# Attention stage: k transposed on TensorE, its high half copied on GpSimd, the first batch's tails turned on TensorE, and the order of the cycle written anew

## The chip, the cores and the metric

One core of one Trainium2 chip runs the whole program. The metric is the device time of one execution in microseconds; the time before is the median of three runs.

## The reference

```
# q, k, v: (2, 8, 576, 64), s: (2, 8, 576)
scores = (q @ k.T) / sqrt(64)
cum    = cumsum(max(s, 0))
bias   = -(cum[:, :, :, None] - cum[:, :, None, :])
scores = where(causal, -1e9, scores + min(bias, 0)); attn = softmax(scores)
x = attn @ v                      # heads side by side: (1152, 512)
h = x @ w_in;  x = (h * cos(h)) @ w_out          # d_ff = 2048
expert = argmax(x @ w_gate); out = gate * (relu(x_e @ w1[e]) @ w2[e])   # 8 experts, F = 1024
```

The change is in the attention stage alone.

## The kernel before

The program has four stages: attention, the first layer (`l1`), the second layer with the routing, and the experts. Float32 products are built from 16-bit parts: a value is split into a high part and a low part, and three products (high x high, high x low, low x high) are added up in PSUM.

Attention works on eight pairs of heads (n = 0 to 7; pairs 0 to 3 are batch 0). A sequence has 576 rows: four full blocks of 128 (`FULL`) and a tail of 64, and the tails of the two heads of a pair share one tile. For the scores, q and k of a pair must lie transposed, in tiles `qT` and `kT` with two chunks. Chunk 0 holds the high part of one operand over the low part (128 rows); chunk 1 holds the high part once more (64 rows) and six bias rows made from the cumulative sum, 70 rows in all (`KB`). The way there, pair by pair: load (`LQK`), split on GpSimd into `parts_` (`K`: a cast for the high part, a subtraction for the low part), transpose by DMA and read the bias rows from a DRAM copy `bt` (`TR`), and copy the high half into chunk 1 by DMA (`DUP`, the function `twice`). The tails of a batch go the same way (`LT`, `KT`, `TT`, `DT`). Pair 0 is different: `a_first` transposes it on TensorE.

The steps of the computation are S (scores), M (mask, scale and row minimum on VectorE), E (exponential on ScalarE), T (transpose of the probabilities on TensorE), C (copy of it out of PSUM), V (times v), N and R (reciprocal of the row sums, spread over the columns by TensorE), X (tail times v), RC, XS, XT, PX (scaling and splitting the result). S4, SD and the steps with 4 in their name treat the tail. Between them stand D, A and W, which decode and load blocks of `w_in` for the first layer.

All engines work through their queues in program order, and the table `CYCLE` is that order: in iteration i, an entry with offset o treats pair i - o. `ONACT` says which copies C run on ScalarE; the others run on VectorE. PSUM has eight banks: two each of "s", "pt", "mm" and "sm".

Of the kernel before, what the change touches and what calls it, by code (L numbers as in the profile page):

```python
# [74 lines left out]
def kernel(ctx, tc, q, k, v, s, w_in, w_out, wg, w1, w2, out, cap, wide):  # L75
# [238 lines left out]
    def pair_more(n):  # L314
        for x, nm in enumerate("qk"):
            twice(att[n][nm + "T"], x)

    def pair_bias(n):
        for x, nm in enumerate("qk"):
            bias_rows(att[n][nm + "T"], x, n, 0, 1, 2 * FULL)  # L320

    def tail_T(ap, b):
        for x, nm in enumerate("qk"):
            tails[b][nm + "T"] = turned(ap, wt[x], nm + "t", NP, 2)

    def tail_more(b):
        for x, nm in enumerate("qk"):
            twice(tails[b][nm + "T"], x)
# [5 lines left out]
    def a_first(ap):  # L334
        d = att[0]
        work_ = (("q", first[0], d["q"], 0), ("k", first[1], d["k"], 1))
        for nm, w_, f, x in work_:
            gate["hi"] = V(nc.scalar.activation, halves(w_[:, 0], x)[0], f, AF.Copy)
        for nm, w_, f, x in work_:
# [991 lines left out]
```

## Time and profile before

| | us |
|---|---|
| median of 3 runs | 466.72 |
| lowest and highest | 463.45, 467.72 |
| the profiled execution | 464.23 |
| its span | 462.4 |
| TensorE matmul, VectorE, ScalarE, GpSimd busy | 411.2, 329.2, 275.8, 127.8 |

The profiled execution's time is 1.83 us longer than its span; times within it are counted from the start of the span. Durations are those of one execution. Busy times of matmuls are modelled at their ends, so neighbouring rows of the time order can overlap a little.

### The profile page before, as it was taken

The numbers are of one execution on the slowest core, as the hardware profiler recorded it, in microseconds if no ns is written. First come the engines' busy times: TensorE is split into PE (matmuls) and PEld (weight loads), VectorE is DVE, ScalarE is ACT, GpSimd is POOL, SyncE is SP. The second block draws the span as 40 slices with busy tenths as digits, with TensorE's granted clock in tenths as the row PEclk, the third lists the DMA queues.
The fourth block names the chain that finished last, engine by engine and source line by source line (L and its number), as shares of the span: only waits on it lengthen the run. The fifth ranks groups of instructions, "written<-read, shape, count | busy, mean of one in ns | idle before, by whom it ended". The sixth has DMA issues, their size and how long they took to land.

```text
span 462.4 us, 10882 instructions
## 1 busy us (share of the span) xinstructions
PE 411.2 (89%) x4032; PEld 288.3 (62%) x4032; DVE 329.2 (71%) x782; ACT 275.8 (60%) x634; POOL 127.8 (28%) x213
## 2 busy tenths in 40 slices
PE   2487988899999897899899999979899999998994
PEld 2256767676765554555444445435698899888962
DVE  6456889899499958988988566466581467667761
ACT  5256786878666766677722543153653576777771
POOL 7533324511244444354520002201002110220221
PEclk9998999999999999999999999989999999998998
DMA  7799988991313995222255756794769678988851
GB/s 162 154 198 182 189 149 172 182 160 48 93 46 103 328 326 179 93 91 69 72 176 183 216 133 133 178 274 123 251 201 237 105 206 310 306 258 283 286 175 45
DMA packets 101208, 81.82 MB, mean 177 GB/s; under 512 B 72834, under 2 KB 81282, under 8 KB 101147
## 3 DMA queue, kind: packets, MB, share of 16 engines
q1 hardware_dynamic: 97835, 76.06, 62.8%
q0 software_dynamic: 2256, 4.73, 3.2%
q8 instruction: 33, 0.54, 0.5%
q10 hardware_dynamic: 1056, 0.26, 0.3%
q14 instruction: 28, 0.23, 0.2%
HBM read 57.67 MB, written 12.36 MB: 151 GB/s over the span
## 4 chain that ended last, share of the span: by engine, by line
PE 32%; DMA 10%; DVE 7%; ACT 3%; issue 3%; POOL 1%; SPq 0%; ACTq 0%; DVEq 0%; POOLq 0%
DMA ws<-in_moe_w_dram 8%; PE ps_mm L813 7%; PE ps_sm L813 4%; PE ps_s L1012 3%; PE ps_pt L990 2%; PE ps_s L990 2%; PE ps_pt L1012 2%; PE ps_mm L990 2%; PE ps_pt L813 2%; PE ps_s L813 2%; PE ps_mm L1012 2%; ACT gall L605 2%; DMA xr<-row 1%; DVE y L764 1%; DVE gall L606 1%
## 5 line engine op out<-in xcount | busy, mean ns | idle before, releaser
L758 PEld LDWEIGHTS <-win 128*128 128x128 f16 x576 | 56.1, 98 | 45.6 <-issue 9.9
L813 PEld LDWEIGHTS <-gall 128*128 128x128 f16 x432 | 41.3, 98 | 50.7 <-issue 4.2
L813 PE MATMUL ps_mm<-wout,gall 128*128 128x512 f16 x240 | 58.0, 387 | 1.3 <-DVE n__2891 L772 1.3
L606 DVE SCALAR_TENSOR_TENSOR gall<-ws,gall 128x1024 f16<-128x1024 f32 x32 | 38.6, 1220 | 21.3 <-ACT gall L605 21.1
L240 ACT ACTIVATE z<-z,st 128x128 f32<-128x128 f32 (+2 forms) x80 | 44.3, 556 | 7.4 <-DVE st L240 7.4
L999 POOL DMA_INDIRECT out_dram<-gall,eM x16 | 20.5, 1282 | 99.1 <-ACT gall L998 90.5
L605 ACT ACTIVATE gall<-ws 128x1024 f16<-128x1024 f32 x32 | 33.6, 1056 | 23.7 <-DMA ws<-in_moe_w_dram 23.6
L240 DVE CUSTOM_DVE_ANT_0 z<-ps_s,zm 128x512 f32<-128x512 f32 (+3 forms) x72 | 34.8, 507 | 14.0 <-PE ps_s L243 13.7
L605 ACT ACTIVATE wout<-ws 128x512 f16<-128x512 f32 (+1 forms) x32 | 27.2, 860 | 26.1 <-DVE ws L636 19.3
L606 DVE SCALAR_TENSOR_TENSOR wout<-ws,wout 128x512 f16<-128x512 f32 (+1 forms) x32 | 30.3, 956 | 9.7 <-ACT wout L605 9.6
L758 PE MATMUL ps_mm<-xT,win 128*128 128x384 f16 x192 | 33.8, 326 | 2.4 <-DVE n__2438 L772 2.0
L758 PE MATMUL ps_s<-xT,win 128*128 128x384 f16 x192 | 34.3, 326 | 1.7 <-DVE n__2257 L772 0.6
L893 POOL DMA_INDIRECT disp<-row,rsli x9 | 9.2, 1021 | 94.6 <-ACT rm L874 48.5
L606 DVE SCALAR_TENSOR_TENSOR win<-ws,win 128x1024 f16<-128x1024 f32 (+1 forms) x27 | 27.1, 1003 | 10.6 <-ACT win L605 10.2
L758 PE MATMUL ps_pt<-xT,win 128*128 128x384 f16 x192 | 33.8, 326 | 0.9 <-DVE n__2555 L772 0.9
L605 ACT ACTIVATE win<-ws 128x1024 f16<-128x1024 f32 (+1 forms) x27 | 24.2, 897 | 16.8 <-DMA ws<-in_moe_w_dram 10.8
L243 PE MATMUL ps_s<-kT,qT 128*128 128x128 f16 (+7 forms) x128 | 26.3, 329 | 5.9 <-DMA kT<-kT 5.2
L246 PE MATMUL ps_pt<-idf,z 128*128 128x128 f32 x192 | 30.0, 289 | 0.1
L240 ACT COPY p<-ps_pt 128x512 f32<-128x512 f32 (+1 forms) x32 | 16.8, 526 | 22.2 <-PE ps_pt L246 21.9
L771 ACT ACTIVATE y<-y,quarter 128x384 f32<-128x384 f32 x48 | 29.1, 606 | 0.0
L990 PEld LDWEIGHTS <-gall 128*128 128x128 f16 x480 | 28.0, 97 | 0.7 <-DVE gall L606 0.5
L246 PEld LDWEIGHTS ps_pt<-idf,z 128*128 128x128 f32 x192 | 22.9, 148 | 5.1 <-issue 2.6
(483 smaller groups left out, 879.6 us busy)
## 6 DMA issues: line engine op xcount, KB each, us to landing
ws<-in_moe_w_dram SPq DMA_DIRECT2D x64, 512.0 KB
ws<-in_moe_w_in_dram SPq DMA_DIRECT2D x16, 512.0 KB
ws<-in_moe_w_out_dram SPq DMA_DIRECT2D x16, 512.0 KB
disp<-zc SPq DMA_DIRECT2D x18, 257.0 KB
out_dram<-zc SPq DMA_DIRECT2D x9, 256.0 KB
qf<-in_q_dram SPq DMA_DIRECT2D x16, 128.0 KB
vf<-in_v_dram SPq DMA_DIRECT2D x16, 128.0 KB
kf<-in_k_dram SPq DMA_DIRECT2D x14, 128.0 KB
```

The costliest lines, as they stand in the source:

```text
L240: return pin(f(*a, **kw))
L243: return pin(nc.tensor.matmul(out_, **kw))
L246: return pin(nc.tensor.transpose(out_, in_, id_))
L605: nc.scalar.activation(hi, src, AF.Copy, scale=sc)
L606: (eng or nc.vector).scalar_tensor_tensor(lo, src, sc, hi, ALU.mult, ALU.subtract)
L758: nc.tensor.matmul(hp[:, 0:CH], lhsT=win[a][:, kk, fs], rhs=xT[:, x_, kk, xs], start=(n == 0), stop=(n == 3 * KD - 1))
L771: nc.scalar.activation(y, y, AF.Sin, scale=TWO_PI, bias=quarter)
L813: gate["pe"] = nc.tensor.matmul(xp, lhsT=G[c][:, a, f, ts], rhs=wout[w_][:, f, :], start=(f == 0 and n == 0), stop=(f == KF - 1 and n == 2))
L893: sc = nc.gpsimd.indirect_dma_start(out=disp, out_offset=bass.IndirectOffsetOnAxis(ap=sli.bitcast(U32), axis=0), in_=r, in_offset=None, bo ...
L990: gate["pe"] = nc.tensor.matmul(hp[:, 0:ns], lhsT=a1[:, kk, a, fs], rhs=X[:, x_ * KD + kk, 0:ns], start=(n == 0), stop=(n == 3 * KD - 1))
L999: sc = nc.gpsimd.indirect_dma_start(out=out, out_offset=bass.IndirectOffsetOnAxis(ap=M[:, b, 1:2].bitcast(U32), axis=0), in_=y, in_offset= ...
L1012: nc.tensor.matmul(yp[:, 0:ns], lhsT=a2[:, f, w_, d * 128:(d + 1) * 128], rhs=Hh[:, a, f, :], start=(n == 0), stop=(n == 3 * KE - 1))
```

## The change

k is no longer transposed by DMA: eight TensorE transposes per pair (`KT`) write one bank of "sm", seen as 1024 16-bit columns, and VectorE copies it to `kT` (`CK`). q stays with the DMA transpose. The second copy of the high half, of q, k and tails, is made by GpSimd instead of DMA. For that the places of the high and the low part are swapped in `halves`, so that q's high part is copied from partitions 64 to 127 and k's from 0 to 63. The tile `kT` has two buffers instead of three. The tails of batch 0 are cast, doubled and transposed in `a_first`, on ScalarE, GpSimd and TensorE, with their bias columns from SBUF; those of batch 1 still go by DMA transpose. The copies C4 and C4b go to ScalarE, and `ONACT` changes. The loads of pair 3 are issued ahead of the loop, and the whole table `CYCLE` is another order.

```
-ONACT = ((0,), (1,), (3, 0), (3, 1))
+ONACT = ((1,), (2, 0), (3, 1))
...
-    ("DUP", -1), ("C", 1, 1), ("DT", -1), ("LQK", -3), ("S", 0, 0, 1), ("S", 0, 0, 0), ("T", 1, 2, 0), ("E4b", 1), ("M", 1, 3, 1),
...
+    ("LQK", -3), ("S", 0, 0, 1), ("C", 1, 2, 1), ("S", 0, 0, 0), ("E", 1, 3, 1), ("S", 0, 1, 0), ("S", 0, 1, 1), ("M4b", 1), ("T", 1, 3, 0),
+    ("PX", 2), ("BK", -1), ("C", 1, 2, 0), ("M", 0, 0, 1), ("M", 0, 0, 0), ("KT", -1), ("E4", 1), ("M", 0, 1, 0), ("C", 1, 3, 0),
...
     def halves(w_, x):
-        return w_[:, :, x, :], w_[:, :, 1 - x, :]
+        return w_[:, :, 1 - x, :], w_[:, :, x, :]
...
     def twice(t, x):
-        V(nc.sync.dma_start, t[0:D, 1], t[x * D:x * D + D, 0])
+        o = (1 - x) * D
+        V(nc.gpsimd.tensor_copy, t[0:D, 1], t[o:o + D, 0])
...
-    def pair_T(ap, n):
-        for x, nm in enumerate("qk"):
-            att[n][nm + "T"] = turned(ap, parts_[x][n % 2], nm, 2 * FULL, PB)
+    def q_T(ap, n):
+        d = att[n]
+        d["qT"] = turned(room(ap, "q", 2 * FULL, PB), parts_[0][n % 2])
+
+    def k_room(ap, n):
+        att[n]["kT"] = room(ap, "k", 2 * FULL, 2)
...
+        for z in tail_:
+            hi_(*z)
+        for z in tail_:
+            lo_(*z)
...
+        for z in tail_:
+            dup_(*z)
+        for c in range(2):
+            for w_, f, x in tail_:
+                turn_(w_, tl["qk"[x] + "T"], c, 0, nc.scalar.copy, i)
+                i += 1
...
     def o_C4(n):
-        V(nc.vector.tensor_copy, d["p4"], d["pt4"])
+        V(nc.scalar.copy, d["p4"], d["pt4"])
...
     def o_TR(n):
         if n > 1:
-            pair_T(pools["ap"], n)
-            pair_bias(n)
+            q_T(pools["ap"], n)
+            pair_bias(n, 0)
+
+    def o_BK(n):
+        if n > 1:
+            k_room(pools["ap"], n)
+            pair_bias(n, 1)
+
+    def o_KT(n):
+        if n:
+            pt = att[n]["ptk"] = bank("sm", 2, F16, 1024)
+            for j in range(2 * FULL):
+                tr_(pt[:, j * 128:(j + 1) * 128], parts_[1][n % 2][:, j].rearrange("p b d -> p (b d)"), idh)
+
+    def o_CK(n):
+        if n:
+            V(nc.vector.tensor_copy, att[n]["kT"][:, 0].rearrange("p a t -> p (a t)"), att[n]["ptk"])
...
+        load(ap, 0, "v", v, 3)
         V(nc.sync.dma_start_transpose, out=bT, in_=bias_)
-        tail_T(ap, 0)
-        load_v(ap, 0)
+        q_T(ap, 1)
+        load_tail(ap, 0, "v", v, 2)
+        wl["load"]()
         V(nc.sync.dma_start, bt[0:NBT * 128, :].rearrange("(b p) t -> p b t", p=128), bT)
-        pair_T(ap, 1)
-        tail_more(0)
-        tail_bias(0)
-        pair_more(1)
-        pair_bias(1)
-        wl["load"]()
+        load_qk(ap, 3)
+        k_room(ap, 1)
+        for x in range(2):
+            pair_bias(1, x)
```

Before, SyncE's queue at the start, behind the first loads (`bT` is the transposed bias block, `wt` the split tails, `parts` the split pair 1):

```order
L240 DMA_TRANSPOSE bT<-bias__101 128x7x128
L240 DMA_TRANSPOSE qtT<-wt_109 128x4x128
L240 DMA_TRANSPOSE ktT<-wt_110 128x4x128
L240 DMA vf<-in_v_dram 128x4x64 x2
L240 DMA vt<-in_v_dram 64x4x64 x2
L240 DMA bt<-bT 128x7x128
L240 DMA_TRANSPOSE qT<-parts_106 128x8x128
L240 DMA_TRANSPOSE kT<-parts_108 128x8x128
L240 DMA qtT<-qtT 64x512
L240 DMA ktT<-ktT 64x512
L240 DMA qtT<-bt 6x4x128
L240 DMA ktT<-bt 6x4x128
```

After, the same place of the same queue, SyncE's at the start:

```order
L240 DMA vf<-in_v_dram 128x4x64 x2
L240 DMA_TRANSPOSE bT<-bias__101 128x7x128
L240 DMA_TRANSPOSE qT<-parts_106 128x8x128
L240 DMA vt<-in_v_dram 64x4x64 x2
L663 DMA ws_91<-in_moe_w_in_dram 128x4x128
L240 DMA bt<-bT 128x7x128
L240 DMA qf<-in_q_dram 128x4x64 x2
L240 DMA kf<-in_k_dram 128x4x64 x2
L240 DMA qT<-bt 6x8x128
L240 DMA kT<-bt 6x8x128
```

Nothing of the tails is left in it; the bias rows of pair 1 stand behind a weight load and the loads of pair 3.

Before, GpSimd in one full cycle (casts and subtractions of the next pair, and the residue of a finished one):

```order
L240 CAST parts_106<-qf 128x8x64
L240 TENSOR_TENSOR parts_106<-qf,parts_106 128x8x64
L240 TENSOR_TENSOR xT<-xs,xT 128x576
L240 CAST parts_108<-kf 128x8x64
L240 TENSOR_TENSOR parts_108<-kf,parts_108 128x8x64
```

After, GpSimd in one full cycle:

```order
L240 TENSOR_TENSOR xT<-xs,xT 128x576
L240 CAST parts_105<-qf 128x8x64
L240 TENSOR_TENSOR parts_105<-qf,parts_105 128x8x64
L240 COPY kT<-kT 64x1024
L240 COPY qT<-qT 64x1024
L240 CAST parts_107<-kf 128x8x64
L240 TENSOR_TENSOR parts_107<-kf,parts_107 128x8x64
```

The two copies of 64x1024 are the former DMA copies, between the split of q and the split of k.

Before, VectorE from the reciprocal of a pair's row sums on (`ws`, `wdec` and `win` are the weight steps D, an ISA row on `z` is M):

```order
L240 TENSOR_TENSOR sm__565<-sm__565 128x1
L240 TENSOR_TENSOR rs<-sm__565,eps 128x9
L240 RECIPROCAL rs<-rs 128x9
L240 COPY p_851<-ps_sm 128x128
L240 ISA z_838,st<-ps_s,zm 128x384
L240 ISA st 128x1
L240 SCALAR_TENSOR_TENSOR ws_92<-ws_92 128x512
L240 TENSOR_SCALAR wdec<-ws_93 128x512
L240 SCALAR_TENSOR_TENSOR ws_93<-ws_93,wdec 128x512
```

After, VectorE from the same reciprocal on:

```order
L240 TENSOR_TENSOR sm__610<-sm__610 128x1
L240 TENSOR_TENSOR rs<-sm__610,eps 128x9
L240 RECIPROCAL rs<-rs 128x9
L240 COPY kT<-ps_sm 128x1024
L240 SCALAR_TENSOR_TENSOR ws_92<-ws_92 128x512
L240 ISA z_883,st<-ps_s,zm 128x512
L240 ISA st 128x1
L240 TENSOR_SCALAR wdec<-ws_93 128x512
L240 ISA z_893,st<-ps_s,zm 128x384
L240 ISA st 128x1
L240 SCALAR_TENSOR_TENSOR ws_93<-ws_93,wdec 128x512
```

The copy of k has come in, a copy of the tail has gone to ScalarE, and the three weight steps stand apart, with a mask step between each two.

## Rows read from the trace of the kernel before

**Rows 1.** Totals by stretch, cut at each start of the sum spread.

```profile
core 0: us, PE busy (x) PEld busy (x) DVE busy (x) ACT busy (x) POOL busy (x), PEclk, DMA share, GB/s
34.41:49.31 14.90, 11.87 (x127) 9.24 (x127) 10.43 (x33) 8.95 (x28) 7.18 (x9) 0.89 0.97 177
49.31:60.22 10.91, 10.30 (x128) 8.09 (x128) 9.79 (x33) 8.95 (x29) 3.87 (x5) 1.00 1.02 193
60.22:73.38 13.16, 10.45 (x127) 8.11 (x127) 10.77 (x33) 10.00 (x30) 4.23 (x5) 1.00 0.76 153
73.38:84.28 10.90, 10.30 (x128) 8.09 (x128) 10.45 (x33) 8.28 (x26) 5.25 (x7) 1.00 0.86 189
84.28:95.96 11.68, 10.38 (x128) 8.12 (x128) 9.66 (x33) 9.23 (x29) 4.92 (x72) 1.00 1.10 150
95.96:107.18 11.22, 10.29 (x129) 8.09 (x128) 10.99 (x37) 9.65 (x32) 1.28 (x1) 1.00 0.63 126
...
119.98:225.40 105.42, 98.94 (x585) 56.81 (x584) 92.04 (x160) 74.52 (x155) 45.47 (x48) 1.00 0.46 144
```

**Rows 2.** TensorE in order of time, start; columns: start, duration, what, idle before.

```profile
12.46 0.63 PE L246 MATMUL ps_pt<-idh,first 128*70 128x128 f16 x4
12.88 0.31 PE L243 MATMUL ps_s<-kT,qT 128*128 128x128 f16 x1
...
17.25 0.31 PE L243 MATMUL ps_sm<-ktT,qtT 128*128 128x128 f16 x1
23.81 0.27 PE L243 MATMUL ps_sm<-ktT,qtT 70*128 70x128 f16 x1 [6.25 <-DMA ktT<-bt]
...
34.41 1.09 PE L243 MATMUL ps_mm<-idf,rs 128*64 128x128 f32 x16 [0.94 <-DVE rs L240]
```

**Rows 3.** TensorE in order of time, the three waits for copied k.

```profile
42.25 0.33 PE L243 MATMUL ps_s<-kT,qT 70*128 70x128 f16 x3 [2.44 <-DMA kT<-kT]
...
67.11 0.33 PE L243 MATMUL ps_s<-kT,qT 70*128 70x128 f16 x3 [1.50 <-DMA kT<-kT]
...
90.97 0.33 PE L243 MATMUL ps_s<-kT,qT 70*128 70x128 f16 x3 [1.30 <-DMA kT<-kT]
```

**Rows 4.** TensorE by microsecond: busy, granted clock, DMA share, GB/s.

```profile
41.00:42.00 1.00, 0.00 (x0) 1.00 0.99 200
...
45.00:46.00 1.00, 1.00 (x6) 0.50 1.13 345
```

**Rows 5.** SyncE's issues by form: duration ns min/median/max, first and last start.

```profile
L240 SPq DMA_TRANSPOSE qT<-parts x7: 1237/1264/1741, 17.7 to 89.2; - x7
L240 SPq DMA_TRANSPOSE kT<-parts x7: 1247/2135/2777, 19.2 to 90.5; - x7
L240 SPq DMA_DIRECT2D qT<-qT x7: 472/509/1277, 22.7 to 95.7; - x7
L240 SPq DMA_DIRECT2D kT<-kT x7: 461/542/595, 23.2 to 97.4; - x7
```

**Rows 6.** VectorE: a 16-bit copy in order of time; copies by form.

```profile
12.70 0.42 DVE L240 COPY kT<-ps_s 70x512 f16<-70x512 f16 x1
...
L240 DVE COPY p<-ps_pt 128x384 f32<-128x384 f32 x4 | 2.2, 555 | 1.3 <-PE ps_pt L246 1.3
L240 DVE COPY p<-ps_pt 128x512 f32<-128x512 f32 x2 | 1.4, 692 | 0.0
L240 DVE COPY p<-ps_sm 128x128 f32<-128x128 f32 x3 | 0.7, 229 | 0.0
```

**Rows 7.** GpSimd and VectorE in order of time.

```profile
71.78 1.27 POOL L240 TENSOR_TENSOR xT<-xs,xT 128x576 f16<-128x576 f32 x1
73.00 0.61 POOL L240 CAST parts<-kf 128x512 f16<-128x512 f32 x1
73.69 1.16 POOL L240 TENSOR_TENSOR parts<-kf,parts 128x512 f16<-128x512 f32 x1
...
49.79 0.69 DVE L240 SCALAR_TENSOR_TENSOR win<-ws,win 128x512 f16<-128x512 f32 x1
...
73.86 1.53 DVE L240 SCALAR_TENSOR_TENSOR win<-ws,win 128x512 f16<-128x512 f32 x1
```

**Rows 8.** ScalarE, copies by form.

```profile
L240 ACT COPY p<-ps_pt 128x512 f32<-128x512 f32 x7 | 4.0, 576 | 0.9 <-PE ps_pt L246 0.8
...
L240 ACT COPY p<-ps_pt 128x256 f32<-128x256 f32 x2 | 0.7, 372 | 2.2 <-PE ps_pt L246 2.2
```

More of the change, by code (lines that the diff above doesn't have):

```diff
@@ L121, with bank @@
     rot = [0]
-    def bank(tag, bufs=2, dt=F32):
-        return ps.tile([128, 512], dt, tag=tag, bufs=bufs, name=f"ps_{tag}")
+    def bank(tag, bufs=2, dt=F32, n=512):
+        return ps.tile([128, n], dt, tag=tag, bufs=bufs, name=f"ps_{tag}")
     def any_bank():
@@ L292, in cast_tails, with room, turned @@
         for x in range(2):
-            cast(wt[x], tails[b]["qk"[x]], x)
-    def turned(ap, w_, nm, nt, bufs):
-        t = ap.tile([128, 2, nt, 128], F16, tag=f"{nm}T", name=f"{nm}T", bufs=bufs)
+            cast(wt[x][:, 0], tails[b]["qk"[x]], x)
+    def room(ap, nm, nt, bufs):
+        return ap.tile([128, 2, nt, 128], F16, tag=f"{nm}T", name=f"{nm}T", bufs=bufs)
+    def turned(t, w_):
         V(nc.sync.dma_start_transpose, out=t[:, 0], in_=w_.rearrange("p a b d -> p (a b d)"))
@@ L308, in bias_rows, with pair_bias @@
         V(nc.sync.dma_start, t[D:KB, 1], bt[o:o + count * step * 6, :].rearrange("(j c) t -> c j t", c=step * 6)[0:6])
-    def pair_T(ap, n):
-        for x, nm in enumerate("qk"):
-            att[n][nm + "T"] = turned(ap, parts_[x][n % 2], nm, 2 * FULL, PB)
[L314 to L320, printed above, removed]
+    def q_T(ap, n):
[3 more added lines that the diff above has]
+        att[n]["kT"] = room(ap, "k", 2 * FULL, 2)
+    def pair_bias(n, x):
+        bias_rows(att[n]["qk"[x] + "T"], x, n, 0, 1, 2 * FULL)
     def tail_T(ap, b):
         for x, nm in enumerate("qk"):
[L324 to L328, printed above, removed]
+            tails[b][nm + "T"] = turned(room(ap, nm + "t", NP, 2), wt[x][:, 0])
     def tail_bias(b):
@@ L334, in a_first, with hi_ @@
     def a_first(ap):
[L335 to L339, printed above, removed]
+        d, tl = att[0], tails[0]
+        work_ = [(first[x], d["qk"[x]], x) for x in range(2)]
+        tail_ = [(wt[x], tl["qk"[x]], x) for x in range(2)]
+        def hi_(w_, f, x):
+            V(nc.scalar.activation, halves(w_[:, 0], x)[0], f, AF.Copy)
@@ L340, in a_first, with lo_, dup_, turn_ @@
+        def lo_(w_, f, x):
             hi, lo = halves(w_[:, 0], x)
             V(nc.gpsimd.tensor_tensor, lo, f, hi, ALU.subtract)
-            V(nc.scalar.copy, w_[:, 1, :, 0, :], hi)
-            d[nm + "T"] = ap.tile([128, 2, 2 * FULL, 128], F16, tag=f"{nm}T", name=f"{nm}T", bufs=PB)
-        for nm, w_, f, x in work_:
+        def dup_(w_, f, x):
+            V(nc.scalar.copy, w_[:, 1, :, 0, :], halves(w_[:, 0], x)[0])
+        def turn_(w_, t, c, a, f, i):
+            pt = bank(*BANKS[i % 3], F16)
+            m = KB if c else 128
+            for j in range(4):
+                tr_(pt[0:m, j * 128:(j + 1) * 128], w_[:, c, a + j, :, :].rearrange("p b d -> p (b d)")[:, 0:m], idh)
+            V(f, t[0:m, c, a:a + 4, :].rearrange("p a t -> p (a t)"), pt[0:m, 0:512])
@@ L347, in a_first @@
         i = 0
         for c in range(2):
-            for nm, w_, f, x in work_:
+            for w_, f, x in work_:
                 for a in (0, 4):
-                    tg, nb = BANKS[i % 3]
-                    pt = bank(tg, nb, F16)
-                    m = KB if c else 128
-                    for j in range(4):
-                        tr_(pt[0:m, j * 128:(j + 1) * 128], w_[:, c, a + j, :, :].rearrange("p b d -> p (b d)")[:, 0:m], idh)
-                    gate["first"] = V(nc.vector.tensor_copy if c else nc.scalar.copy, d[nm + "T"][0:m, c, a:a + 4, :].rearrange("p a t -> p (a t)"), pt[0:m, 0:512])
-                    i += 1
+                    turn_(w_, d["qk"[x] + "T"], c, a, nc.vector.tensor_copy if c else nc.scalar.copy, i)
+                    i += 1
@@ L359 @@
+        for z in tail_:
+            dup_(*z)
+        for c in range(2):
+            for w_, f, x in tail_:
+                turn_(w_, tl["qk"[x] + "T"], c, 0, nc.scalar.copy, i)
+                i += 1
     SC = -0.125
@@ L465, in o_C4b @@
         d["p5"] = tile_("p5", 128)
-        V(nc.vector.tensor_copy, d["p5"], d["pt5"][:, 0:128])
+        V(nc.scalar.copy, d["p5"], d["pt5"][:, 0:128])
     def o_N(n):
@@ L540, in o_TR, with o_DUP @@
         if n > 1:
[L541 to L544 removed]
+            q_T(pools["ap"], n)
+            pair_bias(n, 0)
+    def o_BK(n):
         if n > 1:
[L546 removed]
+            k_room(pools["ap"], n)
[8 more added lines that the diff above has]
+            V(nc.vector.tensor_copy, att[n]["kT"][:, 0].rearrange("p a t -> p (a t)"), att[n]["ptk"])
+    def o_DUP(n, x):
+        if n:
+            twice(att[n]["qk"[x] + "T"], x)
     def o_LT(n):
@@ L562, in o_DT @@
         if n and n % NP == 0:
-            tail_more(n // NP)
+            for x in range(2):
+                twice(tails[n // NP]["qk"[x] + "T"], x)
     pools = {}
@@ L1226 @@
         parts_ = [[ap.tile([128, 2 * FULL, 2, D], F16, name=f"parts{x}{i}") for i in range(2)] for x in range(2)]
-        wt = [ap.tile([128, NP, 2, D], F16, name=f"wt{i}") for i in range(2)]
+        wt = [ap.tile([128, 2, NP, 2, D], F16, name=f"wt{i}") for i in range(2)]
         dm = ap.tile([128, 1], F32, name="dm")
```

19 lines of the change are left out of this document (13 added, 6 removed), and 13 rows, old and new, of the table CYCLE.

## The prediction

> **What bounds the kernel now.** I read the totals by stretch first [rows 1]. TensorE is the fullest engine, but the change touches only the attention stage, which ends at 119.98 us; the first layer behind it lasts 105.42 us and everything later is released by program order and buffers, so what attention gives back I pass on whole. The table is cut at the eight points where TensorE starts the matmuls that spread the row sums of a pair (one such start per cycle, 34.41 the first). In five cycles TensorE is busy 10.30, 10.45, 10.30, 10.38 and 10.29 us: its work per cycle is a constant 10.3. What varies is the rest of the cycle: 0.61, 2.71, 0.60, 1.30 and 0.93 us idle, mean 1.23. VectorE is second (9.66 to 10.99), ScalarE third.
>
> Then TensorE in order of time. At the start it does the dense tail block of pair 0 up to 17.5 us and waits 6.25 us for the bias rows of the tails [rows 2]; in later cycles it waits 2.44, 1.50 and 1.30 us for the copied half of k [rows 3]. After the 2.44 us gap the granted clock stands at 0.50, the lower of its two levels (1.2 GHz) [rows 4], and that cycle has 11.87 us of busy time instead of 10.30 [rows 1]: the gap cost another 1.57. The SyncE queue shows why the copies are late [rows 5]: per pair it issues two transposes (1.26 and 2.14 us), two half copies (0.51 and 0.54), and each copy stands in the queue until its transpose has landed. So DMA, by the order of one queue, holds TensorE at the start and in every other cycle; otherwise TensorE's own work does.
>
> **The change, part by part.** All sums are made against the profiled execution, 464.23 us (span 462.4 and 1.83 around it), which lies 2.49 under the median of three, 466.72.
>
> *Start.* The tails of the first batch are no longer cast by GpSimd, transposed by DMA and copied by DMA; TensorE turns them. That is 16 more transposes ahead of the first scores. A group of four takes 0.43 us from start to start (12.46 to 12.88 [rows 2]), so 4 x 0.43 = 1.7, and I allow 0.4 for the casts and duplicate copies that ScalarE does ahead of them: first scores at 15.0 instead of 12.88. The 6.25 us wait goes. Next late is then the chain scores, mask, exponential, transpose of pair 0, and after it the bias rows of pair 1. Before, from the first scores to the first sum spread took 34.41 - 12.88 = 21.5, or 15.3 without the wait. If only the wait vanished, and both k transposes of this stretch (2 x 0.84, below) were added, it would come at 15.0 + 15.3 + 1.7 = 32.0: the pessimistic end. But 23.81 to 34.41 was no full-rate stretch: every transpose of pair 0 stood in TensorE's queue behind the waiting block, and in the new order they stand ahead of it. Laying the new order out by hand with the rows' durations gives 11.9 us from the first scores, 26.9: the optimistic end, with no semaphore time and nothing late. In the queue the bias rows of pair 1 now stand behind the write of the bias block, one weight load of 512 KB and the loads of pair 3; I put 1 us for that and 1 us for semaphores and take 28.9. That is 5.5 us earlier than 34.41 (ends 2.4 and 7.5).
>
> *Each cycle.* The q transpose stays with DMA. Removed from SyncE: the k transpose and both half copies, 2.14 + 0.51 + 0.54 = 3.2 us of its issue time, and the waits of 2.44, 1.50 and 1.30 us with their cause. Added to TensorE: eight 16-bit transposes a pair, 2 x 0.43 = 0.84 to 0.86. Added to VectorE: one copy of 128x1024 of 16 bits out of PSUM. The nearest row is 0.42 for 512 [rows 6], so 0.8; the ends are 0.69 (a 512 copy of 32 bits) and 1.38 (twice that). VectorE also gains the copies of 256 (0.39, between the rows for 128 and 384) and 512 (0.69), and loses 384 (0.56), 512 (0.69) and 128 (0.23): +0.4 in all. Its own work in the cycle from 73.38 was 10.45, of which 0.84 is one instruction held up beside GpSimd (1.53 instead of 0.69 [rows 7]): 9.6 + 0.4 = 10.0. ScalarE loses 256 and 512, gains 384, 512 and 128: about +0.4 by 0.37 and 0.58 [rows 8], from at most 9.65 to 10.05. Added to GpSimd: two copies of 64x1024. The nearest row is a cast of 512 in 0.61 [rows 7], so about 1.15 each; the ends are 0.6 (as for 512) and 2.3 (at the 1.16 of a two-input operation on 512, twice). GpSimd then has 1.27 for the residue of the finished pair, 2 x (0.61 + 1.16) of casts and 2.3 of copies: 7.1 us.
>
> So TensorE's work becomes 10.3 + 0.85 = 11.15 and no other engine's comes above it. The two copies have time: behind VectorE's copy of k about 6 of the 11.15 us stand in TensorE's queue before the next scores (sum spread, tail, values, four groups of transposes, tail scores; counted from the order), and both copies take 2.3. They would be late only above 3 us each, which no row supports. The wait for the reciprocals (most of 0.61, 0.60 and 0.93) should shrink, as four pieces of TensorE work now stand between the last exponential of the tail and the spread of the sums. I take 0.35 us idle, half of what those cycles show: 11.5 a cycle. From the first sum spread to the sixth there are five such cycles: 57.5 against 14.90 + 10.91 + 13.16 + 10.90 + 11.68 = 61.55, or -4.05. The ends are 55.75 (no idle) and 61.9 (the mean idle of 1.23 stays), -5.8 to +0.35. The sixth interval has no k transpose: 10.3 + 0.5 against 11.22, -0.4. The last stretch to 119.98 I leave as it is.
>
> Sum: -5.5 - 4.05 - 0.4 = -9.95, about **-10 us**: 454.2 for the profiled execution, **456.7** against the median. The ends add up to -2.0 and -14.2.
>
> **A lock between VectorE and GpSimd.** The trace shows a two-input weight step of VectorE taking 1.53 us where it takes 0.69 elsewhere, and a GpSimd subtraction that started 0.17 us before it ran until 74.85 [rows 7]: VectorE waited for GpSimd's end. In the new order the three weight steps of a cycle stand right behind the copy of k, at the time when GpSimd runs its two new copies. With a wait of 0.5 us each VectorE's cycle is 10.0 + 1.5 = 11.5, just what I take for TensorE.
> The Trainium skill says on the page "SBUF — State Buffer", section "SBUF: two separate sides", that VectorE and GpSimd share one pair of ports, that whichever starts first holds it for its whole instruction, and that the other is blocked. By that rule a copy with one input blocks as long as a subtraction does, and each weight step could wait out a whole copy: that is the third rival. The row agrees for a two-input operation of GpSimd; no row here shows a step of VectorE beside a plain 16-bit copy.
>
> **The rivals.**
> *TensorE pays and the stalls come back.* The transposes are added in full, and another late party (the copy of k, a bank still held, a reciprocal) takes the place of DMA, so the idle mean of 1.23 stays: +0.35 over the five cycles, and the start falls between the pessimistic end and mine, -3.5: about -3, 463.5. For it: three of the five cycles show no DMA wait and still 0.6 to 0.9 idle. Against it: the two worst cycles do show one.
> *Everything hides.* No idle and the start at its optimistic end: -13.5 to -14, 453. For it: the work of every other engine is below 11.15. Against it: no cycle before was without a gap.
> *VectorE becomes the bound: slower.* The three weight steps and the two small additions ahead of the reciprocal each wait 0.9 us for a GpSimd instruction (the one in the row waited 0.84): 10.0 + 4.5 = 14.5 a cycle. Five cycles cost 72.5 - 61.55 = +11, the sixth 14.5 - 11.22 = +3.3, the start gives -5.5: +8.8, 475.5. It decides the sign from where these waits, less the 1.15 us that VectorE has to spare, eat the gain over seven cycles: 1.15 + 10/7 = 2.6 us a cycle. Against it: before, with 3.87 to 5.25 us of GpSimd work in the four cycles from 49.31 to 95.96 [rows 1], VectorE stayed at 9.66 to 10.77.
> *The clock falls again.* One more dip such as the one at 45 us costs 1.57; it is in the range and no case of its own.
>
> **How the numbers follow.** A measurement of this kernel can tell about 1% (4.7 us) from no change. I give the forecast (-7 to -12) 0.58, everything hides (-12 to -15) 0.17, the stalls that come back (-5 to 0) 0.17, VectorE as the bound 0.06, and 0.02 to no change from some cause outside. Faster by over 1%: the first two and a share of the third, 0.79; within 1%: 0.15; slower by over 1%: 0.06. The range that leaves out 2 in 10 runs from 452.5 (-14.2) to 462.3 (-4.4).
>
> **What would show it.** Right: first scores near 15 us, no wait for the tails' bias rows, the first sum spread near 29 and the sixth near 86; intervals near 11.5 with TensorE busy near 11.15; the 128x1024 copy near 0.8 and the GpSimd copies near 1.15; no waits of TensorE for DMA behind the first 25 us; the first layer again near 105 us. Wrong: VectorE without idle time while TensorE waits for scores' masks, weight steps of over 1.2 us in each cycle, a wait of over 3 us for the bias rows of pair 1, or a first layer that grows by what attention gave back.

## The result, and the profile after

The changed kernel takes 451.11 us (median of 4 runs, 447.27 to 451.79) beside 465.09 (463.16 to 467.72) for the kernel before: ratio 0.968, 95% interval 0.960 to 0.976. The forecast was 456.7 with a range of 452.5 to 462.3, so the sign was right and the time lies 1.4 us below the range. Of the 5.6 us between forecast and time, 1.6 are the kernel before, whose median came out at 465.09 instead of 466.72; as a gain, 14.0 us against a forecast of 10 and an end of 14.2, it is just inside. The profiled execution has a span of 449.8 us (462.4 before). The profiled executions of the changed kernel (451.79), of order_old (464.99) and of dup2 (461.26) are the longest of their kernels' runs, so whole times are compared by medians and stretches by profiles.

First the totals by stretch, cut as in [rows 1] at each start of the sum spread, and the first layer behind attention (same columns).

```profile
27.67:37.99 10.32, 10.32 (x139) 8.53 (x137) 9.63 (x31) 8.70 (x27) 9.28 (x11) 1.00 0.86 199
37.99:48.60 10.61, 10.55 (x139) 8.57 (x137) 10.42 (x34) 8.88 (x30) 7.60 (x8) 1.00 0.85 139
48.60:59.21 10.61, 10.43 (x140) 8.64 (x138) 10.22 (x33) 9.63 (x32) 9.13 (x10) 1.00 0.87 185
59.21:69.53 10.32, 10.32 (x140) 8.54 (x137) 9.65 (x33) 9.23 (x29) 7.32 (x7) 1.00 0.54 132
69.53:79.97 10.44, 10.41 (x139) 8.55 (x137) 10.32 (x33) 9.05 (x30) 9.09 (x76) 1.00 0.51 130
79.97:90.68 10.71, 10.44 (x131) 8.12 (x129) 10.64 (x36) 9.33 (x31) 3.52 (x3) 1.00 0.18 50
...
104.11:209.00 104.89, 99.93 (x585) 57.44 (x584) 91.98 (x161) 74.36 (x155) 45.00 (x49) 0.98 0.47 147
```

Look at the first two columns: the cycle is 10.32 to 10.61 us long and TensorE is busy for nearly all of it, 52.03 of 52.30 us over the five. VectorE stands just under (9.63 to 10.42). The granted clock is 1.00 in every cycle, where [rows 1] had 0.89 in the first.

TensorE in order of time, the changed start and the only wait for a transfer behind it; these answer to [rows 2, 3].

```profile
13.45 0.63 PE L246 MATMUL ps_pt<-idh,first 128*70 128x128 f16 x4
...
15.15 0.63 PE L246 MATMUL ps_mm<-idh,wt 128*70 128x128 f16 x4
15.58 1.07 PE L243 MATMUL ps_s<-kT,qT 128*128 128x128 f16 x8
...
23.29 0.78 PE L243 MATMUL ps_s<-kT,qT 70*128 70x128 f16 x7 [1.70 <-POOL parts L240]
27.67 1.04 PE L243 MATMUL ps_mm<-idf,rs 128*64 128x128 f32 x16
...
54.83 0.78 PE L243 MATMUL ps_s<-kT,qT 70*128 70x128 f16 x7 [0.18 <-DMA kT<-bt]
```

The 6.25 us wait [rows 2] and the 2.44, 1.50 and 1.30 [rows 3] are gone. A wait of 1.70 is left at the first scores that need the bias rows of pair 1, and 0.18 is all that DMA costs TensorE in the cycles. (The profile puts the 1.70 down to GpSimd. In a second profile of the same kernel, *after_again*, the same wait is 1.95 us and put down to the bias rows, and *rows_first* below removes it by reading them sooner.)

VectorE and GpSimd by form between 27.67 and 90.68 us (columns as in [rows 6]), beside [rows 6 to 8].

```profile
L240 DVE SCALAR_TENSOR_TENSOR ws<-ws,wdec 128x512 int32<-128x512 int32 x5 | 5.0, 997 | 0.0
L240 DVE COPY kT<-ps_sm 128x1024 f16<-128x1024 f16 x5 | 3.2, 632 | 0.0
L240 DVE SCALAR_TENSOR_TENSOR win<-ws,win 128x512 f16<-128x512 f32 x4 | 2.7, 684 | 0.0
L240 POOL COPY kT<-kT 64x1024 f16<-64x1024 f16 x6 | 7.9, 1316 | 8.6 <-DVE kT L240 5.1 <-PE ps_s L243 3.4
L240 POOL COPY qT<-qT 64x1024 f16<-64x1024 f16 x6 | 7.6, 1259 | 0.3
```

Where the time went, from start to start:

| stretch | before | after | difference | forecast |
|---|---|---|---|---|
| to the first sum spread | 34.41 | 27.67 | -6.74 | -5.5 |
| five cycles | 61.55 | 52.30 | -9.25 | -4.05 |
| sixth interval | 11.22 | 10.71 | -0.51 | -0.4 |
| rest of attention (to 119.98, to 104.11) | 12.80 | 13.43 | +0.63 | 0 |
| first layer and all behind it | 342.42 | 345.69 | +3.27 | 0 |
| span | 462.4 | 449.8 | -12.6 | -9.95 |

The five cycles gave 5.2 us more than forecast. Attention as a whole gave 15.9, and the stretch behind it took 3.3 of that back in this execution.

### The profile page after: what moved, and what is told of

It is laid out like the page before. It is cut to its first block, busy times and chain, and to the rows that moved or that the text cites. A ratio compares the mean times of both kernels' runs of the same rounds, so it can differ in the third digit from the quotient of the medians.

```text
span 449.8 us, 11016 instructions
## 1 busy us (share of the span) xinstructions
PE 413.2 (92%) x4104; PEld 295.0 (66%) x4104; DVE 328.8 (73%) x783; ACT 279.7 (62%) x650; POOL 146.4 (33%) x227
## 4 chain that ended last, share of the span: by engine, by line
PE 33%; DMA 9%; DVE 7%; issue 5%; ACT 4%; SPq 2%; POOL 1%; POOLq 0%; ACTq 0%; DVEq 0%
DMA ws<-in_moe_w_dram 8%; PE ps_mm L852 6%; PE ps_sm L852 4%; PE ps_pt L1029 3%; PE ps_mm L1029 3%; PE ps_mm L1051 3%; PE ps_s L1029 3%; PE ps_s L1051 2%; PE ps_pt L1051 2%; PE ps_s L852 2%; PE ps_pt L852 2%; DVE y L803 1%; ACT gall L644 1%; DVE gall L645 1%; DVE ws L674 1%
## 5 line engine op out<-in xcount | busy, mean ns | idle before, releaser
L852 PEld LDWEIGHTS <-gall 128*128 128x128 f16 x432 | 41.3, 98 | 50.7 <-issue 4.2
L797 PE MATMUL ps_mm<-xT,win 128*128 128x384 f16 x192 | 35.5, 337 | 2.3 <-DVE n__2523 L811 2.0
L645 DVE SCALAR_TENSOR_TENSOR win<-ws,win 128x1024 f16<-128x1024 f32 (+1 forms) x27 | 27.8, 1031 | 12.0 <-ACT win L644 11.9
L1029 PEld LDWEIGHTS <-gall 128*128 128x128 f16 x480 | 27.9, 97 | 1.1 <-DVE gall L645 0.7
L246 PE MATMUL ps_pt<-idf,z 128*128 128x128 f32 x192 | 28.1, 279 | 0.5 <-ACT p L240 0.2
L246 PEld LDWEIGHTS ps_pt<-idf,z 128*128 128x128 f32 x192 | 21.1, 141 | 7.9 <-ACT p L240 3.5
L243 PE MATMUL ps_s<-kT,qT 128*128 128x128 f16 (+7 forms) x128 | 23.7, 303 | 2.2 <-POOL parts L240 1.7
L1051 PEld LDWEIGHTS <-gall 128*128 128x128 f16 x384 | 23.7, 100 | 2.9 <-issue 2.9
```

The lines of the kernel that those rows point to most:

```text
L243: return pin(nc.tensor.matmul(out_, **kw))
L246: return pin(nc.tensor.transpose(out_, in_, id_))
L645: (eng or nc.vector).scalar_tensor_tensor(lo, src, sc, hi, ALU.mult, ALU.subtract)
L797: nc.tensor.matmul(hp[:, 0:CH], lhsT=win[a][:, kk, fs], rhs=xT[:, x_, kk, xs], start=(n == 0), stop=(n == 3 * KD - 1))
L852: gate["pe"] = nc.tensor.matmul(xp, lhsT=G[c][:, a, f, ts], rhs=wout[w_][:, f, :], start=(f == 0 and n == 0), stop=(f == KF - 1 and n == 2))
L1029: gate["pe"] = nc.tensor.matmul(hp[:, 0:ns], lhsT=a1[:, kk, a, fs], rhs=X[:, x_ * KD + kk, 0:ns], start=(n == 0), stop=(n == 3 * KD - 1))
```

## The experiments

**Halves of the change.** Two theories went in: that the engines which now turn and copy make the gain, whatever the order, because no transfer is left on TensorE's path; or that the order of the cycle makes it. Four kernels put one part back at a time, and one makes the start's part alone.

*tails_only*: the kernel before, with the start of the changed one.

```
-            cast(wt[x], tails[b]["qk"[x]], x)
+            cast(wt[x][:, 0], tails[b]["qk"[x]], x)
...
+        for z in tail_:
+            hi_(*z)
```

> The kernel before with one part of the change alone: the tails of batch 0 are turned by TensorE in the start, everything else (order, k by DMA, copies by DMA) as before. Theory A (the gain has two parts, the wait at the start and the cycles that the SyncE queue stretched): the 6.25 us wait for the tails' bias rows goes, the first sum spread comes near 30 us instead of 34.41, the five intervals behind it stay within 2 us of 61.55, time about 5 us under before (460). Theory B (the order of the cycle gave nearly all): the first sum spread stays above 32 us, since every transpose of pair 0 still stands behind the tail block, time within 3 us of before.

462.46 us, ratio 0.987 (0.976 to 0.998). First scores at 15.45, the first sum spread at 30.20 instead of 34.41; a wait of 2.42 us for bias rows at 23.30; the five cycles as uneven as before (63.46 in all, with waits of 2.67 and 2.73 us for the copied k). So the start brings the first sum spread 4.2 us forward by itself and needs nothing of the rest; 1.9 of it were lost again in the cycles of this execution, and the interval of the ratio is too wide for a price of the whole.

*order_old*: transposes and copies by TensorE, VectorE and GpSimd and the new `ONACT`, in the order of the cycle before.

```
-    ("LQK", -3), ("S", 0, 0, 1), ("C", 1, 2, 1), ("S", 0, 0, 0), ("E", 1, 3, 1), ...
+    ("C", 1, 1), ("LQK", -3), ("BK", -1), ("S", 0, 0, 1), ("S", 0, 0, 0), ("T", 1, 2, 0), ...
+    ("XT", 2), ("KT", -1), ("T", 1, 3, 1), ("E", 0, 0, 0), ("M", 0, 1, 1), ...
+    ("A",), ("CK", -1), ("DUP", -1, 1), ("DUP", -1, 0), ("DT", -1), ("S", 0, 2, 0), ("N", 1), ...
```

> The changed kernel with the order of the cycle of before (the new steps put in: bias rows of k at the top, k transposes behind XT, copy of k and both half copies behind A), the new ONACT and engines kept. Theory A (DMA and its queue stretched the cycles): the waits of TensorE for DMA are gone with the old order too, five intervals near 55 us (10.3 + 0.45 + 0.3 each), time at most 4 us above the changed kernel (455). Theory B (the order gave the gain of the cycles): five intervals near 60 us, time 8 us or more above the changed kernel (459 or more).

461.13 us, ratio 0.989 (0.984 to 0.994). No wait for DMA in the cycles, and yet they take 61.65 us, as before. The totals of a middle cycle:

```profile
54.88:67.19 12.31, 10.94 (x135) 8.51 (x136) 11.73 (x33) 9.27 (x28) 8.91 (x10) 1.00 0.64 116
```

VectorE's weight steps by form, from 42.57 to 92.49 us:

```profile
L240 DVE SCALAR_TENSOR_TENSOR ws<-ws,wdec 128x512 int32<-128x512 int32 x3 | 3.7, 1246 | 0.1
L240 DVE SCALAR_TENSOR_TENSOR win<-ws,win 128x512 f16<-128x512 f32 x3 | 3.5, 1177 | 0.0
```

TensorE at a sum spread, in order of time:

```profile
79.50 0.77 PE L243 MATMUL ps_mm<-idf,rs 128*64 128x128 f32 x10 [0.96 <-DVE rs L240]
```

VectorE is busy 11.73 of 12.31 us here; the weight steps take 1.25 and 1.18 us, where the changed kernel has 1.00 and 0.68. TensorE waits about 1 us at each sum spread for the row sums. The engines alone do not make the gain: the ratio is that of the start by itself (tails_only, 0.987). *order_old_nod* below shows where the rest of the 12.31 goes.

*dup_dma*, *k_dma* and *mech_old*: the new order, with the half copies by DMA, the transposes of k by DMA, and both.

```
-        V(nc.gpsimd.tensor_copy, t[0:D, 1], t[o:o + D, 0])      # dup_dma, mech_old
+        V(nc.sync.dma_start, t[0:D, 1], t[o:o + D, 0])
...
+            turned(att[n]["kT"], parts_[1][n % 2])              # k_dma, mech_old: in o_BK
-        if n:                                                   # in o_KT and o_CK
+        if n == 1:
```

> The changed kernel with the high halves copied by DMA from the SyncE queue again, in the same places of the order. Theory A (the queue is what stretched the cycles): SyncE waits for VectorE's copy of k in the middle of each cycle with the loads and transposes behind it, the copies land 2 to 3 us later, TensorE waits for them again in most cycles; five intervals 55 to 58 us instead of 52.3, time 3 to 6 us above the changed kernel. Theory B (order): copies issued in mid-cycle land in time, intervals within 1 us of 52.3, time within 2 us.

> The changed kernel with k of pairs 2 to 7 transposed by DMA again, issued at the top of the cycle (pair 1 stays on TensorE); half copies on GpSimd. TensorE has eight transposes less a cycle, VectorE one copy less. Theory A with TensorE as the bound: if the DMA transposes land before the half copies need them, five intervals fall by 4 x 0.45 to 5 x 0.45, to about 50.3, time 1 to 2 us under the changed kernel; if they are late, TensorE waits 1 us or more in several cycles and the time is 2 to 6 us above it. Theory B: within 1 us either way, since neither engine matters.

> The changed kernel's order of the cycle with the transfers of before: k of pairs 2 to 7 transposed by DMA, all high halves copied by DMA (tails of batch 0 still on TensorE). [...] Theory B (the order alone carries the gain): five intervals under 55, time at most 455.

| order | transfers as before | k by DMA only | half copies by DMA only | engines |
|---|---|---|---|---|
| before | 465.09; with the new start (tails_only) 462.46 | - | - | 461.13 |
| new | 467.22 | 460.49 | 467.98 | 451.11 |

All cells but the 465.09 have the new start, and mech_old leaves k of pair 1 on TensorE, so its transfers are not quite those of before. Ratios: dup_dma 1.003 (0.998 to 1.007), k_dma 0.990 (0.981 to 0.998), mech_old 1.005 (1.001 to 1.009). dup_dma came out worse than any number given for it, its five cycles 62.82 us; mech_old took 65.36 (waits of 3.11, 4.39 and 1.70), k_dma 61.28. Two of them lose at the start as well: the copied half of pair 1 is 5.84 us (dup_dma) and 6.59 us (mech_old) late, and the first sum spread stands at 35.26 and 34.21 instead of 27.67. With the transfers at these places the new order by itself gives no gain; other places for them were not tried. The stretches of k_dma show it in one kernel: a cycle with a late transfer, and one without.

```profile
27.33:43.68 16.35, 13.05 (x132) 10.06 (x129) 10.45 (x32) 10.35 (x31) 8.59 (x11) 0.79 0.92 187
43.68:53.99 10.31, 10.20 (x131) 8.07 (x129) 9.57 (x32) 7.56 (x23) 7.72 (x8) 1.00 0.62 119
```

TensorE of the same kernel, in order of time:

```profile
34.63 0.22 PE L243 MATMUL ps_s<-kT,qT 128*128 128x128 f16 x1 [1.32 <-DMA kT<-parts]
36.83 1.35 PE L243 MATMUL ps_s<-kT,qT 70*128 70x128 f16 x7 [1.98 <-POOL qT L240]
```

And by microsecond (columns as in [rows 1]):

```profile
41.00:42.00 1.00, 1.00 (x5) 0.63 (x4) 1.00 (x1) 0.73 (x3) 1.00 (x1) 0.50 1.51 234
```

Waits of 1.32 and 1.98 us are 3.30 us of idle time, but the cycle is 6.04 longer: behind them the granted clock stands at 0.50, the lower of its two levels, from 37 to 42 us, and the same work is busy for 13.05 us instead of 10.20. In dup_dma the order of SyncE's queue makes the operand late again; SyncE's issues, in order of time:

```profile
45.85 0.47 SPq L240 DMA_DIRECT2D kT<-kT  x1
46.85 1.25 SPq L240 DMA_TRANSPOSE qT<-parts  x1
...
53.46 0.51 SPq L240 DMA_DIRECT2D qT<-qT  x1
```

TensorE's longest wait, behind them:

```profile
56.10 1.33 PE L243 MATMUL ps_s<-kT,qT 70*128 70x128 f16 x7 [4.47 <-issue]
```

The copy of q is issued 7.6 us behind that of k. What stands between them belongs to others: the transpose of the next pair's q (46.85; entries `TR` and `DUP` differ by one pair), those of the second batch's tails, bias rows and loads of v. TensorE waits 4.47 us, and that cycle is 17.40 long.

**Prices.** *kt2* doubles the transposes of k, *dup2* the copies of GpSimd; *onact_old* gives the copies of probabilities back to the engines that had them.

```
-            for j in range(2 * FULL):                           # kt2
+            for j in [*range(2 * FULL), *range(2 * FULL)]:
...
+        for _ in range(2):                                      # dup2
             V(nc.gpsimd.tensor_copy, t[0:D, 1], t[o:o + D, 0])
...
-ONACT = ((1,), (2, 0), (3, 1))                                  # onact_old
+ONACT = ((0,), (1,), (3, 0), (3, 1))
-        V(nc.scalar.copy, d["p4"], d["pt4"])                    # p5 likewise
+        V(nc.vector.tensor_copy, d["p4"], d["pt4"])
```

> The changed kernel with the eight transposes of k issued twice in each cycle (the second set writes the same values into the same bank). It prices eight transposes where TensorE's queue is the bound. By the trace of the changed kernel (0.45 us from the first of them to what follows) a cycle grows by 0.45 us, seven of them 3.2 us, if TensorE is the bound without slack; by the price of the prediction (0.85) 6 us; under 1 us if another loop sets the 10.3 us of a cycle.

> The changed kernel with each GpSimd half copy made twice: GpSimd gets 2.2 to 2.7 us more a cycle. If GpSimd's copies hold VectorE's weight steps up and VectorE has no slack, cycles grow by 0.5 us or more (3.5 us in all, or more); if the copies end early enough and VectorE has slack, the time stays within 1.5 us of the changed kernel. The second copy ends about 2.5 us later than the first one now does, against some 3.3 us that lie between its end and the scores that read it (59.21 to 69.53 us of the changed kernel's trace).

> The changed kernel with the copies out of PSUM on the engines of before (C0, C1, C30, C31 on ScalarE; C20, C21, C4, C4b on VectorE). VectorE gets 0.4 us less, ScalarE 0.4 us less a cycle than in the changed kernel. If TensorE is the bound and only sums matter: within 1.5 us of the changed kernel. If places in the order matter (a copy behind a held-up weight step), 0.5 us or more a cycle, 3 us or more in all.

kt2: 449.95 us, ratio 0.966 (0.959 to 0.972), and cycles of 10.77, 10.77, 10.77, 10.78 and 10.77. Sixteen transposes in a row, in order of time:

```profile
59.69 1.06 PE L246 MATMUL ps_sm<-idh,parts 128*128 128x128 f16 x16
60.58 0.49 PE L243 MATMUL ps_s<-kT,qT 128*128 128x384 f16 x2
```

0.89 from start to start, so eight cost 0.445, and the cycle grew by 0.45 over 10.32: in the changed kernel TensorE has no slack, and what is added to its work is added to the cycle. (The time as a whole does not show it. In the profiled execution attention ended 5.3 us later than in the changed kernel, 3.5 of them at the start, and the stretch behind it was 3.8 us shorter.)

dup2: 456.71 us, ratio 0.979 (0.970 to 0.987); cycles of 10.85, 11.38, 14.24, 10.33 and 10.66, with 2.08 us of TensorE waiting for GpSimd's parts in the third. GpSimd has less to spare than its busy time says, since what it does next is the casts that TensorE's transposes read. onact_old: 454.51 us, 0.972 (0.961 to 0.982), an interval that takes in the changed kernel's ratio; but its cycles are 11.04 to 11.69 without one wait of TensorE over 0.5 us: 0.77 a cycle more, in short waits. By the cycles, where the copies stand is part of the gain.

**The start.** *rows_first* lets the bias rows of pair 1 go ahead of a weight load and the loads of pair 3; *warm* gives TensorE 17 matmuls of zeros that nobody reads, ahead of the sum transposes and between the first transposes; *warm_rows* does both; *rows_ahead* adds the same for the later pairs and leaves the weight load ahead of the loop out.

```
-        wl["load"]()                                            # rows_first
-        load_qk(ap, 3)
...
+        wl["load"]()
+        load_qk(ap, 3)
...
+                f(nc.tensor.matmul(hotp, lhsT=hot[:, 0:128], rhs=hot, start=True, stop=True))   # warm
...
-    ("LQK", -3), ("S", 0, 0, 1), ...                            # rows_ahead
+    ("BK", -1), ("LQK", -3), ("W",), ("LT", -3), ("S", 0, 0, 1), ...
```

> The changed kernel with SyncE's queue at the start in another order: the bias block's write and the bias rows of pair 1 ahead of the weight load and the loads of pair 3. If the 1.7 us wait of TensorE at 23.29 us is for those rows, it goes or falls under 0.5, the first sum spread comes 1 to 1.5 us earlier (26.2 to 26.7), time 1 to 1.5 us under the changed kernel. If the wait is for GpSimd (casts and copies of pair 1), it stays.

> The changed kernel with 17 added matmuls of zeros of 128x512 in TensorE's idle time at the start (8 before the first transposes of the sums, 3 behind them, 6 between the two chunks of pair 0); nobody reads what they write. If the transposes of the start take 0.43 us a group of four because TensorE had stood idle, the later groups fall to 0.22, the first scores come 1.3 to 1.7 us earlier (near 14), and the time falls by up to 1.5 us unless the bias rows of pair 1 then stand for longer. If the rate does not come from idleness, the groups stay at 0.43 and the time stays.

> Both of the edits above together: if each stands for what it should, first sum spread near 25 us and time 2 to 3 us under the changed kernel (0.4 to 0.7%), the fastest version here.

> The version with the zero matmuls at the start and the bias rows of pair 1 ahead, and now also the bias rows of each later pair, and the loads of q and k, ahead of the weight load and the tails' loads of a cycle (the weight load ahead of the loop left out). If the waits of 3.25 and 4.56 us for the rows of pair 2 in those two versions come from the loads ahead of them in the DMA queues, they go; first sum spread near 25, five intervals near 52.5, attention 2.5 us shorter than in the changed kernel, time 2 to 3 us under it. If the rows are late for another reason, the wait stays and the time is that of the changed kernel.

rows_first: 453.57 us (0.974, 0.971 to 0.978); first sum spread 0.86 earlier, but the wait comes back at pair 2 (3.25 us for bias rows at 36.10), and that cycle is 16.24 long. warm: 450.40 (0.966, 0.962 to 0.970). Its transposes go at twice the rate, in order of time:

```profile
13.05 0.39 PE L248 MATMUL ps_s<-idh,wt 128*128 128x128 f16 x4
13.28 0.39 PE L248 MATMUL ps_pt<-idh,wt 128*70 128x128 f16 x4
...
13.72 0.44 PE L245 MATMUL ps_s<-kT,qT 128*128 128x128 f16 x2
```

A group of four takes 0.22 us from start to start instead of 0.43, and the first scores come at 13.72, 1.86 us sooner. All of it is lost again: TensorE waits 3.05 us for the same bias rows, the granted clock then stands at 0.50 from 23 to 26 us, and the first sum spread comes at 28.80, 1.1 us later than in the changed kernel. warm_rows: 451.48 (0.971, 0.968 to 0.974), a first sum spread at 25.02, and 4.56 us of waiting at pair 2. rows_ahead: 451.04 (0.971, 0.965 to 0.976), waits of 1.91 and 1.33 us elsewhere. Each moves the wait; none beats the changed kernel beyond what a measurement can tell.

**What was still open**: whether VectorE's weight steps are what holds order_old, whether TensorE alone holds the new cycle, and whether the longer stretch behind attention belongs to the change. *order_old_nod* is order_old with the weight steps (`("A",)` and three `("D",)`) taken out of the cycle; *kt_half* makes four of the eight transposes; *after_again* is the changed kernel once more.

```
-            for j in range(2 * FULL):                           # kt_half
+            for j in range(2 * FULL if n == 1 else FULL):
```

> The old order with the new engines, and the weight steps D and A taken out of the cycle (their work is done in one piece behind attention, so that the output is the same). If VectorE, with its weight steps held up beside GpSimd, set the 12.3 us of a cycle in that kernel, the cycles fall to 10.3 to 10.9 us and VectorE's busy time to under 10; if the order itself sets it, they stay above 11.5. The decoding then stands in the open behind attention: some 8 to 12 us there.

> The changed kernel with only four of the eight transposes of k for pairs 2 to 7 (both heads get the first head's k in the first chunk, so the scores of the second head are not those of the reference); VectorE copies the same 1024 columns in two pieces. If TensorE's own work is the 10.3 us of a cycle, cycles fall by 0.22, five intervals by 1.1 us, to 51.2. If another loop sets 10.3 us once TensorE has a little less (as the cycles of 10.31 us in the kernel without k transposes suggest), they stay at 52.3, and a cycle of before, without k transposes, was not bound by TensorE's work but by that loop.

> The changed kernel once more, unaltered, as the measure for the run next to it and for what lies behind attention. If the 3.3 us more behind attention in its first profile belong to the change, this profile shows 345 us there again; if they are the clock of that execution, it shows 341 to 342, as most of the other kernels do.

order_old_nod (one execution, 469.09 us, since the steps then run later) has four cycles of 11.74 to 11.75 and one of 12.17; a stretch of it:

```profile
54.00:66.00 12.00, 10.81 (x145) 8.77 (x143) 9.27 (x32) 9.14 (x29) 8.14 (x10) 1.00 0.45 102
```

VectorE is busy only 9.27 of 12 us, and the cycle is still 1.4 above the new one: the weight steps cost 0.57 of the 12.31. Most of the rest stands at the sum spread, which waits 1.08 to 1.19 us for the row sums. VectorE and GpSimd of order_old_nod, in order of time, show what these wait for:

```profile
61.12 1.27 POOL L240 TENSOR_TENSOR xT<-xs,xT 128x576 f16<-128x576 f32 x1 [3.58 <-ACT xT L240]
61.23 1.18 DVE L240 TENSOR_TENSOR sm__799<-sm__799 128x1 f32<-128x1 f32 x1
62.34 0.61 POOL L240 CAST parts<-kf 128x512 f16<-128x512 f32 x1
62.52 0.46 DVE L240 TENSOR_TENSOR rs<-sm__799,eps 128x9 f32<-128x9 f32 x1
```

The same two additions in the changed kernel:

```profile
57.51 0.29 DVE L240 TENSOR_TENSOR sm__816<-sm__816 128x1 f32<-128x1 f32 x1
57.84 0.17 DVE L240 TENSOR_TENSOR rs<-sm__816,eps 128x9 f32<-128x9 f32 x1
```

In the old order each small addition ahead of the reciprocal starts beside a GpSimd instruction and ends within 0.04 us of it (62.41 and 62.39, 62.98 and 62.95). Together they take 1.18 us more than in the changed kernel, as much as the wait. The kernel before has it too: 0.48 and 1.14 us for the two, ahead of its wait of 1.22 at 73.38. So a part of what the new order does is to let GpSimd subtract the residue elsewhere. This is read from the rows; no run moved the residue alone.

kt_half: 458.24 us, and cycles of 10.39, 10.46, 10.31, 10.31 and 10.52, not shorter. TensorE in order of time in one of them:

```profile
55.55 0.39 PE L246 MATMUL ps_sm<-idh,parts 128*128 128x128 f16 x4
56.11 1.25 PE L246 MATMUL ps_pt<-idf,z 128*128 128x128 f32 x8
```

The 0.22 us saved comes back in the transposes of the probabilities, eight of which take 1.25 instead of 1.04. The cycles of k_dma without a late transfer, with no transposes of k at all, also take 10.31. So a second loop stands at 10.31. By its place it goes through the banks of the probabilities' transposes and the copies that clear them; that was not shown by a run of its own. (kt_half leaves transposes out, so its values differ, and with them what the layers behind attention are given; its whole time is no measure.)

after_again: 450.20 us (0.966, 0.960 to 0.970), cycles summing to 51.97 with the first sum spread at 27.47; 448.4 of span, of which 344.8 behind attention.

## Why the prediction was wrong, point by point

*What bounds it.* Right: with the transfers gone TensorE's work is the cycle. kt2 shows it from above, where added work lengthens the cycle in full; kt_half and k_dma add that another loop stands right beneath, so that less work does not shorten it.

*The cycle, 11.5 us*: the failed step. It was 10.3 of work + 0.85 of transposes + 0.35 idle, and measured 10.46.

The 0.85 was mis-priced. The eight transposes were taken from the start [rows 2], where four take 0.43; TensorE of the changed kernel in the cycle:

```profile
66.21 0.61 PE L246 MATMUL ps_sm<-idh,parts 128*128 128x128 f16 x8
66.65 0.49 PE L243 MATMUL ps_s<-kT,qT 128*128 128x384 f16 x2
66.98 1.04 PE L246 MATMUL ps_pt<-idf,z 128*128 128x128 f32 x8
67.86 0.27 PE L246 MATMUL ps_sm<-idf,z 128*128 128x128 f32 x1
```

Eight take 0.44 from start to start, half as much, and kt2 confirms it. That is 0.4 x 5 = 2.0 of the 5.2.

The 10.3 was not work alone. Ends of matmuls are modelled, so a short wait inside a group counts as busy. Eight transposes of probabilities took 1.06 us in a cycle of the kernel before, from start to start, and 0.88 above:

```profile
81.69 1.23 PE L246 MATMUL ps_pt<-idf,z 128*128 128x128 f32 x8
82.75 0.49 PE L243 MATMUL ps_s<-kT,qT 128*128 128x384 f16 x2
```

The sum spread took 1.03 from start to start (73.38 to 74.41), and 0.87 in the changed kernel (59.21 to 60.08). A gapless cycle of 10.32 less the 0.45 leaves 9.87 of work at most: 0.43 a cycle too much, 2.1 in five; 0.34 of the 0.43 is seen in these two places, the rest was not traced. The idle term measured 0.14 over 10.32 instead of 0.35: 1.1. The direction was right there, but not the size: with the additions ahead of the reciprocal hardly held up any more, no wait is left at the sum spread. Together 2.0 + 2.1 + 1.1 = 5.2. The end for no idle, 55.75, took the first two as certain and was therefore no end at all.

*The start, -5.5*: right in its mechanism, -6.74 in size. The 16 transposes cost 1.70 as taken (13.88 to 15.58); what stands ahead of them 1.0 instead of 0.4; from the first scores to the first sum spread it was 12.09 us, near the 11.9 laid out by hand, though the wait for bias rows took 1.70 of it instead of 1. The second us, for semaphores, was not needed, and the hand layout itself held 1.5 too much.

*VectorE and GpSimd.* The copy of k took 0.63 (taken: 0.8, with a lower end of 0.69), GpSimd's copies 1.32 and 1.26 (taken: 1.15, inside the given ends). VectorE as the bound did not come in the new order, but a milder form of it did in order_old. There the weight steps stretched to 1.25 and 1.18 us beside GpSimd's subtractions and copies, VectorE was busy 11.73 of 12.31 us, and 0.57 of the cycle was due to them; the two small additions that the third rival named took 0.95 and 0.46 there, against 0.29 and 0.17 in the changed kernel. In the changed kernel the steps with two inputs on integers still take 1.00. The Trainium skill's rule ("SBUF — State Buffer", section "SBUF: two separate sides": VectorE and GpSimd share a pair of ports, whose holder keeps it for the whole instruction) agrees with these rows; what it costs here was set by where the steps stood.

*The stalls that come back* (463.5) is near what order_old measured, 461: without the new order the row sums take DMA's place. *Everything hides* (-13.5 to -14, 453) has the measured gain almost to the number, and by luck: its terms were -7.5 at the start and -5.8 in the cycles, where the profile has -6.74 and -9.25, with 3.9 lost again behind the sixth interval. *The clock*: I counted a dip as no case of its own; in k_dma and dup_dma the same work was busy 2.85 and 2.49 us longer behind waits of 3.30 and 4.47, and part of the gain is the first cycle's, at 0.89 before and 1.00 after.

*The rest at nothing.* The first layer took 104.89 us (105.42 before), as forecast. What lies behind it was 3.8 longer, at a granted clock of 0.96 instead of 0.98. Nearly all of that is TensorE's busy time (221.23 against 217.86 us), not idle time. The stretch from the first layer on took 337.5 (warm_rows) to 345.9 us (order_old) in the profiles of the kernels whose code there is the same; it goes mostly with the granted clock of the execution (0.99 and 0.98 in these two, 0.97 in the changed kernel), and kt2, rows_first and rows_ahead, close kin of the changed kernel, have 341.9 to 342.5. Both profiles of the changed kernel itself were long, 345.7 and 344.8. Whether that is chance or the change stays open.

## What to carry to other kernels

Price an instruction from a row of the stage to which it goes, and work from start to start: the same transposes cost twice as much at the start, and modelled busy time held waits. An order and the engines that it was laid out for are one change: here the engines in the old order gave 1.1% with the start in it, the new order with nearly the transfers of before lost 0.5%, and both together gave 3.2%. Look at what runs beside a small instruction that much work waits for: two additions of 0.3 and 0.2 us cost over a microsecond a cycle where they stood beside GpSimd's subtraction and cast. Where one engine is gapless, ask what the next loop beneath it is before cutting its work further, and what the clock does behind a gap before allowing one.
